# An adaLN block on one core: the order of the projection's passes, planes kept in SBUF, and weight tiles in ten slots

## The chip, the cores and the metric

The kernel runs on one core of a Trainium2 chip. The metric is the device time of one execution in microseconds. A core has five engines that take their instructions in order and meet by semaphores: TensorE (PE, with its weight loads PEld), VectorE (DVE), ScalarE (ACT), GpSimd (POOL) and SyncE (SP), which issues nearly all transfers (DMA) here. SBUF is the on-chip memory, PSUM the accumulator that TensorE writes.

## The reference, cut to what matters

```python
mod = (silu(c) @ w_mod).reshape(1, 6, 1, -1)          # sa, ca, ga, sb, cb, gb
h = layernorm(x) * (1 + ca) + sa
q = (h @ wq) -> 32 heads of 128;  k, v = last 512 keys of 16 cached heads, each for 2 query heads
o = softmax(q k^T / sqrt(128)) v
x = x + ga * (o @ wo)                                  # wo: 4096 x 576
h = layernorm(x) * (1 + cb) + sb
x = x + gb * ((sigmoid(h @ w_gate) * (h @ w_up)) @ w_down)   # 576 -> 4608 -> 576
```

x is 2048 rows of 576, in float32. Every matrix product is made of three products of rounded halves (hi·lo + lo·hi + hi·hi).

## The kernel before

The 2048 rows are four blocks of 512 rows (`xs[0]` to `xs[3]`, four tiles of 128 rows each). Blocks 0 and 1 are pair 0, blocks 2 and 3 pair 1.

**Attention.** 128 block-heads (a block of rows and a head) of four steps each: N = 512 steps, and the table `seq` sets their order; the second half of them, from step n1 = 256 on, treats blocks 2 and 3. A step n makes scores (`st`), their maximum (`neg`), the exponential (`pp`, with its sum), the transposed probabilities split into halves (`ptt`), a quarter of the next q projection (`qp`) and a quarter of the product with v (`ot`). After a block-head's fourth step 1/sum (`rs`) is written to `rscr` in DRAM and read back, spread over all partitions, as `rb` (`put_rs`, `get_rs`); `ov` is `ot` times `rb`, and `put_o` stores it in `oscr`. Work to be done at a given step is entered with `at_n` (ahead of the step's own work) or `at_late` (behind it).

**Beside attention.** The norm of blocks 2 and 3 (`norm_block`, lines from `n1` on: statistics, then a chain of twelve small operations for 1/sqrt, `ln_rsqrt`, then `ln_apply` with GpSimd multiplying by `scale` and adding `shift`). Four modulation rows (`mod_fetch`, `mod_sum`, `mod_make2`). And background jobs, which use the four blocks' rooms in SBUF to combine and split the weights and store them in DRAM: `wsc` and `dsc` for the MLP, `wosc` for the projection.

**Projection.** o @ wo for a pair is computed by a seven-product scheme of Strassen's kind over 2 x 2 halves. A visit takes 8 heads (q, 0 to 3), a pair and a tile t: four sums of o's planes on GpSimd (`v_sum`), seven splits (`v_split`: `vh`, ScalarE and VectorE), and seven stages of 12 matmuls, each closed by one VectorE addition to x (`x<-a,x`, `x<-b,x`, `x<-c,x`; the letter is the PSUM bank). There are 32 visits; q is the outer loop, then the pair, then t. A set of 8 heads has seven weight tiles of 1.18 MB, in eleven slots (`WSLOT`, b0 to b4 and c0 to c5); four sets, 28 loads. `beside(v, s)` says what is issued beside stage s of visit v, its loads included.

**Last visits and MLP.** Pair 0 is complete after visit 28 of 32, counted from 1. In the last four visits its second norm is made (two chains of 13 for blocks 0 and 1, `early_norm`, `early_scale`, `early_sums`), its seven sums (planes B11 to T4) are written to `scr[0]` and read again as `ts` or into xs, and transposed and split (`load_combo`) into `hc`. The MLP then runs u = 0 to 71 (pair 0: 36, pair 1: 36) with seven products of 7 matmuls (`product`; `sr` is the raw weight, `sw` the split one) and the down products (`down`, with `sd`).

**What sets the order.** `pin` and `keep_order` hold an instruction in the order in which it is written on its engine; the rest is placed by a scheduler that knows the dependences. All instructions are issued through the wrapper `Ordered`, so the profile puts them all on line 36, and they are told apart by the names of their tiles.

Of the kernel before, what the change touches and what calls it, by code (L numbers as in the profile page):

```python
# [9 lines left out]
F32 = mybir.dt.float32  # L10
# [34 lines left out]
def adaln_block_kernel(ctx: ExitStack, tc: tile.TileContext, x, k_cache, v_cache, wq, wo, w_gate, w_up, w_down,  # L45
# [85 lines left out]
    ones = wp.tile([P, P], F32, name="ones")  # L131
# [4 lines left out]
    def mod_rows(tag, pool):  # L136
        return pool.tile([P, D], F32, tag=tag, name=tag)

    def mod_load(m):
# [6 lines left out]
        t = wp.tile([TAIL, D], F32, tag="h", name="wmt", bufs=4)  # L146
# [3 lines left out]
    def mod_sum(loaded):  # L150
        ws, t = loaded
        for j in range(2):
            parts = [ws[j][:, k, :] for k in range(NC)] + [t[:, j * D2 : (j + 1) * D2]]
            for k, w in enumerate(parts):
                keep_order(nc.scalar.activation(w, w, AF.Copy, scale=cexp[: w.shape[0], k : k + 1]))
            for w in parts[1:]:
                kk = w.shape[0]
                nc.gpsimd.tensor_add(parts[0][:kk], parts[0][:kk], w)
# [17 lines left out]
    def ln_stats(b, t, hold=False):  # L176
        if t == 0:
            LN[b] = [const.tile([P, TPB, 2], F32, tag="mv", name="mv", bufs=2),
                     const.tile([P, TPB], F32, tag="ln_y", name="ln_y", bufs=2)]
# [8 lines left out]
    def ln_rsqrt(b, part=None, hold=False):  # L188
        mv, y = LN[b][:2]
        if not part:  # L190
            v = const.tile([P, TPB], F32, tag="ln_v", name="ln_v", bufs=2)
            a = const.tile([P, TPB], F32, tag="ln_a", name="ln_a", bufs=2)
            LN[b] += [v, a]
            i = nc.vector.tensor_scalar(v, mv[:, :, 1], EPS, None, op0=OP.add)
            if hold:
                pin(i)
            yi, vi = y.bitcast(I32), v.bitcast(I32)
            nc.vector.tensor_scalar(yi, vi, 1, None, op0=OP.logical_shift_right)
            nc.vector.tensor_scalar(yi, yi, -1.0, float(0x5F3759DF), op0=OP.mult, op1=OP.add)
        v, a = LN[b][2:]  # L200
        for _ in range(3 if part is None else 1):
            nc.vector.tensor_mul(a, y, y)
            nc.vector.scalar_tensor_tensor(a, a, -0.5, v, op0=OP.mult, op1=OP.mult)
            nc.vector.scalar_tensor_tensor(y, a, 1.5, y, op0=OP.add, op1=OP.mult)
# [110 lines left out]
    def ln_ready(b, part=None):  # L315
        ln_rsqrt(b, part)
        if part not in (None, 2):
            return
# [1088 lines left out]
```

## Time and profile before

| | us |
|---|---|
| three runs | 3102.99, 3108.08, 3110.74 (median 3108.08) |
| profiled execution | 3107.64 |
| its span | 3105.9 |
| TensorE busy | 3028.0 (97%) |
| VectorE busy | 2184.5 (70%) |
| ScalarE, GpSimd busy | 1680.7 and 1682.8 (54% each) |
| mean granted TensorE clock | 0.991 |

Attention lasts until about 1444 us, the projection until about 1835 us, the MLP until the end. The granted clock is the share of its full clock that TensorE was given in a stretch. A line of waits names the engine and what it was about to write, then the engine and tile it waited for. In a timeline a row is a start, a length, the engine, the line, the operation, its output and inputs with their shapes, and in brackets the idle time before it and what ended it.

### The profile page before, as it was taken

The page shows a single profiled execution, that of the slowest core. Times are in us where ns is not written, and L with a number is a line of the kernel's source. Part 1 is how long each engine was busy: PE and PEld are TensorE (multiplying, and loading weights), DVE is VectorE, ACT ScalarE, POOL GpSimd, SP SyncE. Part 2 cuts the span into 40 slices and gives each one's busy share as a digit, 9 for nine tenths or more (in the row PEclk, how much of TensorE's full clock was granted, in tenths as well). Part 3 has the DMA queues.
Part 4 walks back from the last instruction along what each step waited for, and adds up shares of the span by engine and source line. Part 5 has one row for each costly group of instructions (what it writes and reads, how often), then busy time and mean ns, then how long its engine had stood idle before and what let it go on. Part 6 is the DMA issues. An engine that isn't in the chain of part 4 may idle for free.

```text
span 3105.9 us, 49158 instructions
## 1 busy us (share of the span) xinstructions
PE 3028.0 (97%) x16635; PEld 2602.8 (84%) x16635; DVE 2184.5 (70%) x3866; ACT 1680.7 (54%) x3356; POOL 1682.8 (54%) x1556
## 2 busy tenths in 40 slices
PE   8999999989999999998999989999999999999998
PEld 6878788867888888887999977888888888888887
DVE  6666666687666666665888977666666776666668
ACT  5666667746667666654343444444454544444543
POOL 2344458744577763112555546666666575655654
PEclk9999999999999999999999999999999999999999
DMA  3677777667677777547545565545545565455453
GB/s 114 186 193 201 203 228 253 227 193 186 198 257 241 249 242 182 145 122 230 186 159 185 175 207 177 167 137 167 180 135 151 163 187 144 138 150 144 139 157 103
DMA packets 471406, 559.27 MB, mean 180 GB/s; under 512 B 51569, under 2 KB 425073, under 8 KB 465649
## 3 DMA queue, kind: packets, MB, share of 16 engines
q1 hardware_dynamic: 470544, 556.11, 60.3%
q8 instruction: 132, 2.16, 0.3%
q14 instruction: 122, 0.99, 0.1%
q10 hardware_dynamic: 608, 0.00, 0.0%
HBM read 384.44 MB, written 171.54 MB: 179 GB/s over the span
## 4 chain that ended last, share of the span: by engine, by line
PE 86%; DVE 5%; DMA 3%; POOL 2%; issue 1%; ACT 1%; SPq 1%; ACTq 0%; DVEq 0%; POOLq 0%
PE a L36 19%; PE st L36 17%; PE qp L36 12%; PE w L36 12%; PE ot L36 10%; PE c L36 10%; PE b L36 5%; DVE x L36 1%; SPq L36 1%; POOL x L36 1%; POOL hl L36 1%; DMA sr<-wsc 1%; DMA raw<-in_A_wq_dram 0%; POOL vs L36 0%; DVE vh L36 0%
## 5 line engine op out<-in xcount | busy, mean ns | idle before, releaser
L36 DVE TENSOR_TENSOR x<-w,x 128x288 f32<-128x288 f32 x980 | 436.4, 453 | 295.6 <-PE w L36 291.8
L36 PE MATMUL a<-hc,sw 128*128 128x512 f32 x2016 | 584.9, 394 | 12.9 <-POOL sw L36 6.5
L36 PEld LDWEIGHTS w<-sd,hl 128*128 128x128 f32 x3036 | 510.7, 188 | 95.4 <-DVE x L36 8.2
L36 PE MATMUL w<-sd,hl 128*128 128x288 f32 x3036 | 563.8, 295 | 6.6 <-DVE x L36 3.7
L36 DVE TENSOR_REDUCE neg<-st 128x1 f32<-128x512 f32 x512 | 352.2, 688 | 283.8 <-PE st L36 283.2
L36 ACT ACTIVATE ptt<-st 128x512 fp32r<-128x512 f32 x512 | 306.2, 598 | 415.1 <-PE st L36 414.9
L36 PE MATMUL ot<-ptt,vs 128*128 128x512 f32 x1536 | 487.0, 425 | 2.5 <-DVE ptt L36 2.4
L36 PE MATMUL st<-kt,qt 128*128 128x512 f32 x1536 | 444.7, 395 | 2.7 <-ACT pp L36 2.7
L36 PE MATMUL qp<-hTm,wa 128*128 128x512 f32 x1536 | 443.6, 397 | 3.8 <-DVE hTm L36 1.9
L36 DVE TENSOR_TENSOR ptt<-st,ptt 128x512 fp32r<-128x512 f32 x512 | 351.7, 687 | 125.5 <-ACT ptt L36 125.1
L36 ACT ACTIVATE sw<-sr 128x384 fp32r<-128x384 f32 x504 | 261.1, 521 | 264.9 <-issue 88.9
L36 PEld LDWEIGHTS a<-hc,sw 128*128 128x128 f32 x2016 | 355.4, 188 | 54.9 <-POOL sw L36 8.1
L36 ACT ACTIVATE pp<-st,neg 128x512 f32<-128x512 f32 x512 | 350.6, 685 | 45.9 <-DVE neg L36 45.4
L36 POOL TENSOR_TENSOR sw<-sr,sw 128x256 fp32r<-128x256 f32 x252 | 205.3, 816 | 307.0 <-ACT sw L36 212.3
L36 PEld LDWEIGHTS qp<-hTm,wa 128*128 128x128 f32 x1536 | 285.0, 189 | 72.7 <-DVE qt L36 6.9
L36 PEld LDWEIGHTS st<-kt,qt 128*128 128x128 f32 x1536 | 288.3, 189 | 68.1 <-ACT pp L36 4.1
L36 PEld LDWEIGHTS st<-ident,pp 128*128 128x128 f32 x2048 | 254.6, 140 | 85.9 <-issue 11.0
L36 PE MATMUL st<-ident,pp 128*128 128x128 f32 x2048 | 308.5, 273 | 13.8 <-DVE rs L36 10.8
L36 POOL TENSOR_TENSOR x<-x 128x256 f32<-128x256 f32 (+3 forms) x334 | 246.8, 758 | 138.2 <-DMA x<-in_B_w_up_dram 88.3
L36 PE MATMUL c<-hc,sw 128*128 128x512 f32 x1008 | 303.2, 394 | 2.0 <-ACT v L36 2.0
L36 PEld LDWEIGHTS ot<-ptt,vs 128*128 128x128 f32 x1536 | 253.1, 191 | 30.1 <-DVE ptt L36 4.3
L36 POOL TENSOR_TENSOR wa<-raw,wa 128x512 fp32r<-128x512 f32 (+1 forms) x128 | 112.2, 876 | 255.8 <-ACT wa L36 221.9
(173 smaller groups left out, 4750.6 us busy)
## 6 DMA issues: line engine op xcount, KB each, us to landing
sr<-wsc SPq DMA_DIRECT2D x504, 192.0 KB
sd<-dsc SPq DMA_DIRECT2D x249, 288.0 KB
dsc<-x SPq DMA_DIRECT2D x34, 1008.0 KB
rb<-rscr SPq DMA_DIRECT2D x128, 256.0 KB
oscr<-ov SPq DMA_DIRECT2D x64, 512.0 KB
vr<-oscr SPq DMA_DIRECT2D x32, 1024.0 KB
wsc<-x SPq DMA_DIRECT2D x36, 896.0 KB
wosc<-x SPq DMA_DIRECT2D x32, 1008.0 KB
```

The source lines that it names most:

```text
L36: i = got(*args, **kw)
```

## The change

1. **Passes.** `PASSES` names (q, pair): (0,0), (0,1), (1,1), (1,0), (2,0), (3,0), (3,1), (2,1). Pair 0 is complete after 24 visits (`DONE0`; visits are counted from 0 from here on). Set 2 is loaded twice: five sets (`WQ`), 35 loads. Pair 0's norm follows in visits 21 to 30: one chain of 13 operations for both blocks (`ln_some`, two per stage), then ten stages for each tile. From visit 25 on two of the four plane sums of a visit are VectorE's.
2. **Planes.** T1, T2 and T4 go to six `ts` tiles, the other four planes lie in xs. `scr[0]` is gone, and with it its stores and loads. The first two combinations are made in visits 30 and 31, and the first eight `sr` loads and four splits stand there.
3. **Ten slots.** Weight tiles live in a0, a1 (a0 is the four `h` rows, a1 the rows `scale`, `shift`, `gate1`, `gate`, all 576 wide), b0 to b2, c0, c1, d0 to d2. A tile is `[P, 4, 2, D2]`, and `wosc` is stored in that order by set and product, so a load reads 9216 contiguous bytes a partition and a store writes pieces of 1152 bytes (8064 before). Set 0's first two tiles are loaded at steps N − 34 and N − 32, three more at N − 6 to N − 4, the last two behind attention. At a set's end four of the next set's seven tiles are loaded as its stages free them, three two visits earlier. The down weights `sd` use seven of the eight rows later.
4. **Last two block-heads.** 1/sum is spread by TensorE: `ident` times `rs` on VectorE (four 128x128), four matmuls with `ones`, one copy on ScalarE. The last `put_o` is issued by ScalarE.
5. **Norm of blocks 2 and 3.** Statistics and loads some steps earlier, the twelve chain operations one per step. The last loads of x come 18 or more steps earlier.
6. **Modulation sums** one row chunk per step instead of all in one.

The diff, cut to its core:

```diff
-    def mod_sum(loaded):
+    def mod_sum(loaded, k):
...
+    def ln_some(b, both, lo, hi, hold=False):
+        for op in ln_chain(b, both)[lo:hi]:
+            i = op()
             if hold:
                 pin(i)
...
-            at_late(n - 1, put_rs, b)
-            at_late(n + 1, get_rs, b)
+            if b < NBLK - 2:
+                at_late(n - 1, put_rs, b)
+                at_late(n + 1, get_rs, b)
+            else:
+                spread_rs(b)
+                at_late(n - 1, spread_mm, b)
...
+    def spread_rs(b):
+        DG[b] = at.tile([P, TPB, P], F32, tag="qt", name="dg", bufs=2)
+        for i in range(TPB):
+            nc.vector.tensor_scalar(DG[b][:, i], ident, RS[b][:, i : i + 1], None, op0=OP.mult)
+
+    def spread_mm(b):
+        p = ps_qp()
+        for i in range(TPB):
+            nc.tensor.matmul(p[:, i * P : (i + 1) * P], ones, DG[b][:, i], start=True, stop=True)
+        RB[b] = at.tile([P, BLK], F32, tag="rb", name="rb", bufs=2)
+        keep_order(nc.scalar.activation(RB[b], p, AF.Copy))
...
-        at_n(N // 2 - 38 + b, load_x, b)
+        at_n(N // 2 - 43 + b, load_x, b)
     for b in range(NB):
-        at_n(N - 30 + 5 * b, load_x, b)
+        at_n(N - 48 + 4 * b, load_x, b)
...
-        at_n(n_stats + TPB, ln_rsqrt, b)
+        for k in range(12):
+            at_n(n_stats + TPB + k, ln_some, b, False, k, k + 1)
...
-    norm_block(2, n1 - 28, n1 - 20, n1 - 14, 2, scale, shift, nc.gpsimd, nc.gpsimd)
-    norm_block(3, n1 - 24, n1 - 8, n1 - 6, 2, scale, shift, nc.gpsimd, nc.gpsimd)
+    norm_block(2, n1 - 35, n1 - 19, n1 - 14, 2, scale, shift, nc.gpsimd, nc.gpsimd)
+    norm_block(3, n1 - 26, n1 - 9, n1 - 6, 2, scale, shift, nc.gpsimd, nc.gpsimd)
...
-    wosc = [dram.tile([P, 2, 4, 7, D2], F32, tag=f"wosc{q}", name=f"wosc{q}") for q in range(H // 8)]
+    wosc = [dram.tile([7, P, 4, 2, D2], F32, tag=f"wosc{q}", name=f"wosc{q}") for q in range(H // 8)]
...
+    PASSES = (0, 0), (0, 1), (1, 1), (1, 0), (2, 0), (3, 0), (3, 1), (2, 1)
+    WQ = 0, 1, 2, 3, 2
+    WOF = 0, 0, 1, 1, 2, 3, 3, 4
...
+    WSLOT = (("a0", "a1", "b0", "b1", "b2", "d0", "d1"), ("d2", "c0", "c1", "a0", "a1", "b0", "b1"),
+             ("b2", "d0", "d1", "d2", "c0", "c1", "a0"), ("a1", "b0", "b1", "b2", "d0", "d1", "d2"),
+             ("c0", "c1", "a0", "a1", "b0", "b1", "b2"))
...
+        eng = nc.vector if v > DONE0 and k % 2 else nc.gpsimd
...
+        if k in (0, 5):
+            v_load(k // 5)
+        if k in (1, 2, 3):
+            w_load(0, k + 1)
+        if 2 <= k < 6:
+            v_sum(0, k - 2)
+        if k in (6, 7, 8):
+            v_split(0, k - 6)
+
+    for s in range(2):
+        at_n(N - 34 + 2 * s, w_load, 0, s)
...
+        k = WOF[v // TPB]
+        if k + 1 < len(WQ):
+            if v == LAST[k] and s < 4:
+                w_load(k + 1, s + 3)
+            elif v == LAST[k] - 2 and s in (1, 3, 5):
+                w_load(k + 1, s // 2)
+        if DONE0 - 4 < v <= DONE0 and s in (0, 2):
+            ln_stats(s // 2, v - DONE0 + 3)
+            park_x(s // 2, v - DONE0 + 3)
+        if v < DONE0:
             return
-        k = 7 * (v - first - 4) + s
...
+        k = 7 * (v - DONE0) + s
+        if 3 <= k < 10:
+            ln_some(0, True, 2 * (k - 3), 2 * (k - 2), True)
+        for t in range(TPB):
+            at = k - 10 - 10 * t
             if at == 0:
                 early_norm(t)
...
+            if at in (1, 3):
+                early_scale(t, at // 2)
+            if 4 <= at < 8:
+                early_sum(t, at - 4)
...
+        if k in (36, 39, 42, 45):
+            split_w()
+            load_w(True)
+        if k in (47, 51):
+            early_stage((k - 47) // 4)
+            load_combo(0, (k - 47) // 4, True)
```

How the order moves, at three places. VectorE near the norm of block 3 in mid-attention, before: the end of the chain (`ln_a`, `ln_y`), which stands in one piece, and the step's work behind it.

```order
L36 SCALAR_TENSOR_TENSOR ln_y<-ln_a,ln_y 128x4
L36 TENSOR_TENSOR ln_a<-ln_y 128x4
L36 SCALAR_TENSOR_TENSOR ln_a<-ln_a,ln_v 128x4
L36 SCALAR_TENSOR_TENSOR ln_y<-ln_a,ln_y 128x4
L36 TENSOR_TENSOR ov<-ot,rb 128x4x128
L36 TENSOR_TENSOR ptt<-st,ptt 128x4x128
L36 RECIPROCAL rs<-sum 128x4
L36 TENSOR_TENSOR ptt<-st,ptt 128x4x128
```

The same engine after the change, between two `ptt`:

```order
L36 TENSOR_SCALAR h<-x_103,mv,ln_y 128x576
L36 TENSOR_REDUCE neg<-st 128x1
L36 SCALAR_TENSOR_TENSOR ln_y<-ln_a,ln_y 128x4
L36 TENSOR_TENSOR ov<-ot,rb 128x4x128
L36 TENSOR_TENSOR ln_a<-ln_y 128x4
L36 TENSOR_SCALAR h<-x_103,mv,ln_y 128x576
L36 SCALAR_TENSOR_TENSOR ln_a<-ln_a,ln_v 128x4
L36 SCALAR_TENSOR_TENSOR ln_y<-ln_a,ln_y 128x4
L36 TENSOR_TENSOR ln_a<-ln_y 128x4
L36 SCALAR_TENSOR_TENSOR ln_a<-ln_a,ln_v 128x4
L36 SCALAR_TENSOR_TENSOR ln_y<-ln_a,ln_y 128x4
L36 TENSOR_REDUCE neg<-st 128x1
```

The chain is cut up by `neg`, `ov` and the `h` that GpSimd multiplies next, and five of its operations still stand together.

SyncE at the end of attention, before (`wb`, `wc` are weight tiles, `vr` the planes of o for a visit):

```order
L36 DMA wb_15318<-wosc_354 128x8x288
L36 DMA rscr_285<-rs 128x4
L36 DMA wb_15353<-wosc_354 128x8x288
L36 DMA rb<-rscr_285 128x512
L36 DMA oscr_3_293<-ov 512x1x256
L36 DMA wb_15380<-wosc_354 128x8x288
L36 DMA wb_15395<-wosc_354 128x8x288
L36 DMA oscr_3_293<-ov 512x1x256
L36 DMA vr<-oscr_0_286 128x2048
L36 DMA wc_15415<-wosc_354 128x8x288
L36 DMA wc_15417<-wosc_354 128x8x288
```

and after:

```order
L36 DMA rb<-rscr_280 128x512
L36 DMA vr<-oscr_0_283 128x2048
L36 DMA wb_15292<-wosc_350 128x2304
L36 DMA wb_15313<-wosc_350 128x2304
L36 DMA wb_15336<-wosc_350 128x2304
L36 DMA vr<-oscr_0_283 128x2048
L36 DMA oscr_3_290<-ov 512x1x256
L36 DMA wd_15437<-wosc_350 128x2304
L36 DMA wd_15439<-wosc_350 128x2304
```

The last two round trips of 1/sum and the last store are gone from this queue, three weight tiles and both `vr` stand ahead of the last store on it, and two tiles (`wd`) behind.

SyncE at the start of the MLP, before:

```order
L36 DMA ts<-scr_294 128x576 x4
L36 DMA scr_294<-x_101 128x288
L36 DMA scr_294<-x_102 128x288 x2
L36 DMA scr_294<-x_101 128x288
L36 DMA sr<-wsc_300 128x384 x4
L36 DMA x_101<-scr_294 128x576 x4
L36 DMA x_102<-scr_294 128x576 x4
L36 DMA ts<-scr_294 128x576 x2
L36 DMA sr<-wsc_300 128x384 x2
L36 DMA sr<-wsc_301 128x384
```

and after, behind the last three weight tiles of the last set:

```order
L36 DMA wb_18985<-wosc_352 128x2304
L36 DMA wb_19005<-wosc_352 128x2304
L36 DMA wb_19026<-wosc_352 128x2304
L36 DMA sr<-wsc_296 128x384 x4
L36 DMA vr<-oscr_2_289 128x2048 x2
L36 DMA sr<-wsc_296 128x384 x2
L36 DMA sr<-wsc_297 128x384
L36 DMA sr<-wsc_296 128x384
```

The stores to and loads from `scr` are gone, and the MLP's weights (`sr`) stand ahead of the last two `vr` instead of behind them.

More of the change, by code (lines that the diff above doesn't have):

```diff
@@ L1031, in load_sd @@
             g, a = sd_uses[i]
-            t = fpool["p"].tile([P, 2, D2], F32R, tag="sd", name="sd", bufs=7)
+            t = flat(const, (["h"] * 4 + ["scale", "shift", "gate1"])[i % 7])
             d = nc.sync.dma_start(f32(t), dsc[g % NG][:, :, a if g == GL else WITH[a]])
@@ L1212, in beside @@
-        if k == 23:
-            for i in range(4):
-                stage_first(i)
-        if k == 26:
-            load_combo(0, 0, True)
+            if at in (1, 3):
+                early_scale(t, at // 2)
+            if 4 <= at < 8:
+                early_sum(t, at - 4)
+        if v == LAST[3] and s == 6:
+            dctx.close()
+            fpool["s"] = ctx.enter_context(tc.tile_pool(name="fs", bufs=1, side="right", reuse_waits="tile"))
+            for _ in range(4):
+                load_w(True)
```

266 lines of the change are left out of this document (119 added, 147 removed).

## The prediction

> **What bounds the kernel now.** I read the page's busy line first, then the windows of 100 us, then the waits of TensorE.
>
> ```profile
> span 3105.9 us, 49158 instructions
> PE 3028.0 (97%) x16635; PEld 2602.8 (84%) x16635; DVE 2184.5 (70%) x3866; ACT 1680.7 (54%) x3356; POOL 1682.8 (54%) x1556
> ```
>
> TensorE is busy for 97% of the span. The change leaves its matmuls as they are (but for eight small ones), so it can win only holes: 3105.9 − 3028.0 = 78 us, and what a lower granted clock costs behind them. The windows (columns: window, length, busy us of PE, PEld, DVE, ACT, POOL, granted clock, DMA share, GB/s) show where they are:
>
> ```profile
> 100.00:200.00 100.00, 97.38 (x500) 79.52 (x498) 65.35 (x104) 65.09 (x147) 43.54 (x56) 1.00 0.74 199
> 600.00:700.00 100.00, 88.25 (x442) 71.77 (x441) 77.80 (x142) 54.53 (x118) 51.88 (x50) 0.95 0.69 198
> 1400.00:1500.00 100.00, 90.39 (x531) 80.36 (x530) 66.04 (x100) 40.63 (x81) 30.47 (x21) 0.93 0.72 234
> 1700.00:1800.00 100.00, 92.22 (x675) 91.24 (x673) 93.69 (x165) 41.33 (x64) 57.28 (x39) 0.98 0.47 163
> 1800.00:1900.00 100.00, 87.78 (x499) 76.88 (x499) 72.16 (x139) 48.02 (x87) 41.97 (x50) 0.95 0.62 201
> ```
>
> Four windows lose 8 to 12 us each: the norm in mid-attention (B), the passage from attention to projection (C), the projection's last visits (D1) and the MLP's start (D2). Elsewhere a window loses 0 to 4. The longest entry of TensorE's waits (us in total, times, longest) is VectorE's, in B:
>
> ```profile
> PE st L36 <- DVE rs L36: 10.8, 2, 9.8
> ```
>
> **B, the norm in mid-attention.** VectorE and GpSimd here:
>
> ```profile
> 663.44 0.16 DVE L36 TENSOR_SCALAR ln_y<-ln_v 128x4 int32<-128x4 int32 x1
> ...
> 676.09 0.56 DVE L36 TENSOR_SCALAR h<-x,mv,ln_y 128x576 f32<-128x576 f32 x1
> ...
> 678.58 1.33 DVE L36 TENSOR_SCALAR ln_y<-ln_v 128x4 int32<-128x4 int32 x1
> ```
> ```profile
> 676.73 3.15 POOL L36 TENSOR_TENSOR h<-h,scale 128x576 f32<-128x576 f32 x2 [4.51 <-DVE h L36]
> 679.85 2.74 POOL L36 TENSOR_TENSOR h<-h,shift 128x576 f32<-128x576 f32 x2
> ```
> ```profile
> 665.00:670.00 5.00, 3.02 (x17) 1.82 (x15) 4.88 (x11) 1.25 (x3) 3.59 (x3) 1.00 1.00 273
> ...
> 675.00:685.00 10.00, 4.17 (x21) 3.10 (x18) 9.68 (x15) 1.74 (x5) 8.19 (x8) 0.90 0.15 44
> 685.00:690.00 5.00, 1.06 (x5) 1.09 (x6) 4.90 (x10) 0.00 (x0) 4.76 (x7) 0.50 0.11 37
> ```
>
> The same 128x4 operation takes 0.16 us alone and 1.33 us while GpSimd multiplies h. Block 3's twelve stand in one row; TensorE idles 1.98 + 5.83 + 3.94 = 11.75 us. The Trainium skill, "SBUF — State Buffer", section "Who interferes with whom", says that VectorE and GpSimd share one port pair, which an instruction locks to its end. The trace agrees (0.16 against 1.33), and by that rule spreading the chain helps only where GpSimd is not at work beside it: the sum would be that of the upper end below.
>
> The change issues the chain one operation per step. But the order of VectorE that results still has ten chain operations (block 2's tail, block 3's head), four h, two neg, one ptt, one qt and one ov between two ptt, and GpSimd's eight h operations belong to just these four h. At most eight chain operations can each meet one of them: 8 × 1.33 + 2 × 0.16 = 11.0; h 4 × 0.56 = 2.2; neg, ptt and qt 4 × 0.69 and ov about 1.1 = 3.9. Sum 17 us.
>
> ```profile
> L36 DVE TENSOR_REDUCE neg<-st 128x1 f32<-128x512 f32 x512 | 352.2, 688 | 283.8 <-PE st L36 283.2
> ```
> ```profile
> 32.60 0.69 DVE L36 TENSOR_REDUCE neg<-st 128x1 f32<-128x512 f32 x1 [1.09 <-PE st L36]
> ...
> 1434.41 1.07 DVE L36 TENSOR_TENSOR ov<-ot,rb 128x512 f32<-128x512 f32 x1
> ...
> 1437.20 0.67 DVE L36 TENSOR_REDUCE neg<-st 128x1 f32<-128x512 f32 x1
> ```
>
> One neg is one step: 512 of them from 32.6 to 1437.2 us make 2.75 us a step. The 17 us serve two steps, and one step of slack lies in the buffers: stall 17 − 8.25 = 8.8 us. None stretched: 7.7 us of work, no stall. I take the upper end, since the order puts them side by side: **gain 3** (11.75 − 8.8), bounds −1 (block 2's tail stretched before it as well) and +12.
>
> **C, attention to projection.** The chain of waits, then the windows:
>
> ```profile
> 1439.18 4.81 DMA rscr<-rs
> ...
> 1444.06 4.35 DMA rb<-rscr
> ...
> 1450.99 10.03 DMA vr<-oscr
> ```
> ```profile
> 1430.00:1440.00 10.00, 9.09 (x52) 7.18 (x51) 9.54 (x16) 7.32 (x19) 5.48 (x4) 1.00 0.66 194
> 1440.00:1450.00 10.00, 6.79 (x40) 5.57 (x38) 3.49 (x6) 1.71 (x3) 0.00 (x0) 1.00 1.01 303
> 1450.00:1470.00 20.00, 14.51 (x63) 12.88 (x64) 7.03 (x13) 3.04 (x5) 5.38 (x4) 0.66 1.06 383
> ...
> 1475.00:1775.00 300.00, 300.00 (x2252) 300.00 (x2251) 261.83 (x401) 118.90 (x188) 166.61 (x107) 1.00 0.54 182
> ```
>
> In the steady projection a matmul takes 300/2252 = 0.133 us, a visit (84) 11.2 us. The 63 matmuls of 1450–1470 are worth 8.4 us, so 11.6 are lost there; with 0.9 and 3.2 ahead, 15.7. The last head's 1/sum goes out and back (9.3 us with its issue), `ov` waits for it, and behind `ov` on VectorE stand the first x and vh of the projection. SP's queue is held by the same trip, so weights and the second vr come late, all at once.
>
> The change fetches two of seven weight tiles some 90 us earlier, in eight pieces, where the DMA has room:
>
> ```profile
> 1300.00:1400.00 100.00, 100.00 (x515) 82.24 (x514) 68.52 (x107) 60.19 (x133) 11.58 (x13) 1.00 0.42 112
> ```
>
> Their rows (h, scale, shift, the gates) were last read by the background jobs and by the norm of mid-attention, so SP, behind which the next heads' rscr and rb stand, should not be held. The change also replaces the round trip of the last two block-heads by four 128x128 products on VectorE (each between the 0.16 and the 0.56 above, say 0.35), four matmuls and one copy on ScalarE:
>
> ```profile
> L36 PE MATMUL st<-ident,pp 128*128 128x128 f32 x2048 | 308.5, 273 | 13.8 <-DVE rs L36 10.8
> L36 ACT ACTIVATE ptt<-st 128x512 fp32r<-128x512 f32 x512 | 306.2, 598 | 415.1 <-PE st L36 414.9
> ```
>
> 1.4 + 0.6 + 0.6 = 2.6 us instead of 9.3, or up to 1.33 × 4 + 1.2 = 6.5 if GpSimd's sums of the first planes meet the products. What remains: two tiles (d0, d1) can only be fetched when attention's pools close. At 383 GB/s a tile of 1.18 MB takes 3.1 us; behind the last `oscr` store d1 lands some 10 to 13 us after the first stage and is due after 9.6: 3 us late. With 2 for the spread and 2 for the clock, 7 stay. **Gain 8.5**, bounds 4 and 13.
>
> **D1, the last visits.**
>
> ```profile
> 1775.00:1835.00 60.00, 47.84 (x326) 46.09 (x324) 51.25 (x92) 22.86 (x35) 29.95 (x27) 0.94 0.46 150
> ```
> ```profile
> 1789.63 3.45 DVE L36 TENSOR_TENSOR x<-x,scale 128x576 f32<-128x576 f32 x2
> ...
> 1801.54 0.74 DVE L36 TENSOR_TENSOR x<-x,scale 128x576 f32<-128x576 f32 x1
> ...
> 1806.69 0.46 DVE L36 TENSOR_TENSOR x<-x 128x288 f32<-128x288 f32 x1 [1.43 <-POOL x L36]
> ```
> ```profile
> L36 DVE TENSOR_TENSOR vh<-vr,vh 128x512 fp32r<-128x512 f32 x108 | 109.2, 1011 | 6.3 <-ACT vh L36 4.8
> ```
>
> 326 matmuls are worth 43.4 us: 16.6 lost. VectorE is busy without a gap while the norm of pair 0 is pressed into four visits. Its steady load is 261.8 us over 2252/84 = 26.8 visits, 9.8 of 11.2 us. The change has eight visits for this work: one chain of 13 operations in place of two (2 per stage in visits 24 and 25), then one tile in 10 stages. Per tile VectorE gets one scale (0.74) and four sums (0.46), 2.6 us in 1.43 visits: 1.8 a visit. It also takes two of four plane sums from GpSimd (about 0.67 each, as a vh alone): 1.3. On the other side vh's mean 1.01 contains contention: 7 × (1.0 − 0.67) = 2.3 us a visit, of which half should go with GpSimd's two sums. 9.8 + 1.8 + 1.3 − 1.2 = 11.7 against 11.2: VectorE is just over, half a us for each of six visits, and about 2 in visit 24 with the chain. Residue 5, bounds 1 and 12; **gain 11.5**, bounds 5 and 16. What is late next is the x add on which stage 2's bank waits: TensorE has one stage, 1.6 us, of slack against it.
>
> **D2, the MLP's start.**
>
> ```profile
> 1835.00:1877.00 42.00, 34.23 (x175) 27.68 (x174) 26.47 (x49) 24.49 (x46) 12.25 (x20) 0.93 0.67 223
> ```
> ```profile
> 1867.08 0.53 SPq L36 DMA_DIRECT2D sd<-dsc  x1
> 1867.71 2.69 SPq L36 DMA_DIRECT2D sr<-wsc  x3
> ```
> ```profile
> PE c L36 <- ACT v L36: 2.0, 1, 2.0
> PE a L36 <- ACT sw L36: 1.5, 1, 1.5
> ```
>
> Idle 7.8, clock 0.07 × 42 = 2.9: 10.7. Before, SP stores and reloads the planes, then waits for a down weight's slot until 1867 with four MLP weights behind it. After, planes stay, eight weights come and four are split in the visits, two combinations of seven are made there, and the slot's wait stands later. Five combinations with their ScalarE and VectorE copies stay in u = 0, and so does part of those waits. **Gain 7.5**, bounds 3 and 11.
>
> **The rest.** Spread modulation sums: 100–200 lost 2.6 us, gain 1.5 (0 to 3). Pair switch with six ts tiles: 0 (−3 to +2). `wosc` stores in pieces of 1152 bytes where 8064 lay in one: 0, beside a DMA that is 0.7 busy in attention (a loss of up to 4 if that cover goes). The seven extra weight tiles are 8.3 MB, on a DMA that is 0.54 busy (1475–1775): 0, but see rival 1. Each of these loads waits on SP for a stage of the visit before, and behind it stands a vr that is due two visits later.
>
> Sum: 3 + 8.5 + 11.5 + 7.5 + 1.5 = 32. The profiled execution took 3107.6 (span 3105.9 and 1.7 around it), 0.5 under the median of the runs: **3075.6, say 3075 us**.
>
> **Rivals.** (1) Late weights, ending slower. At each of four set changes four tiles are fetched only as the last visit frees them, with a vr ahead: 4.72 + 1.05 = 5.77 MB, from 1.6 us into that visit to stage 6 of the next, 19.2 us. That needs 300 GB/s. At the steady 182 GB/s it takes 31.7: 12.5 late, four times 50, result 3125. For it: before, no set was fetched so late. Against: the same queue moved 383 GB/s in 1450–1470, in smaller pieces. (2) VectorE stays the bound in the last eight visits: D1's gain falls away, 3087. For it the sum of 11.7 against 11.2, against it the halved contention. (3) All holes close, B's too: 3075.6 − 8.8 (B) − 7 (C) − 4 (most of D1's rest) = 3056. For it, that the chain was spread; against, VectorE's order. (4) The change does not do what it says in mid-attention: that is already in B.
>
> **How the numbers follow.** My forecast 0.74, (1) 0.06, (2) 0.12, (3) 0.08. Squares of the half-ranges (6, 5, 5, 4, 3) make ±11 around it; with rivals 2 and 3 the range is 3054 to 3097. Against 0.3% (9 us, what a measurement of this kernel can tell from no change), the bound of faster is 3099: the forecast nearly always, rivals 2 and 3 all but always: 0.90. Same 0.05 (forecast at its worst, rival 1 in part), slower 0.05.
>
> **What would show it.** B: neg and ptt without a gap of TensorE near 680 would refute the 8.8; 128x4 operations of 1.3 us confirm it. C: no `rb<-rscr` on the last chain, first visit in under 19 us, waits on wd. D1: VectorE over 95% from the 25th visit on, PE at 0.133 us a matmul but for some 5 us. D2: no ts or x loads, waits on ACT alone. Rival 1 would show as PE waiting for wa or wb every four to eight visits. The prediction is wrong if less than 10 us of the sum comes.

## The result, and the profile after

The changed kernel takes 3082.56 us (median; runs 3081.02, 3083.32, 3081.80 and 3084.14), the kernel before 3109.35 beside it. The ratio is 0.9918, its 95% interval 0.9901 to 0.9935: 25 us faster by the ratio, 27 by the two medians, where 33 had been forecast (3075, range 3054 to 3097). Variants ran on several chips, each beside the kernel before, so they are compared by these ratios; in one run below (all plane sums on VectorE and the norm on GpSimd) the profile fell into an execution in which TensorE was granted a clock of only 0.85 throughout, and no stage of it is read.

The page after, busy line and span:

```profile
span 3079.0 us, 49150 instructions
PE 3022.5 (98%) x16651; PEld 2600.9 (84%) x16651; DVE 2190.9 (71%) x3872; ACT 1680.2 (55%) x3358; POOL 1641.9 (53%) x1534
```

The windows of 100 us that answer to those shown of before (columns: window, length, busy us of PE, PEld, DVE, ACT, POOL, granted clock, DMA share, GB/s):

```profile
100.00:200.00 100.00, 99.51 (x510) 81.49 (x509) 66.72 (x105) 65.85 (x149) 43.42 (x57) 1.00 0.71 191
600.00:700.00 100.00, 92.42 (x459) 75.05 (x458) 76.58 (x146) 53.79 (x120) 38.44 (x42) 0.97 0.66 181
1400.00:1500.00 100.00, 94.90 (x618) 86.96 (x617) 77.80 (x119) 42.62 (x82) 36.65 (x26) 0.98 0.47 167
1700.00:1800.00 100.00, 89.38 (x643) 85.79 (x642) 91.77 (x164) 41.25 (x66) 35.59 (x27) 1.00 0.49 180
1800.00:1900.00 100.00, 97.65 (x563) 85.82 (x562) 78.53 (x158) 55.47 (x103) 51.78 (x57) 1.00 0.51 162
```

Three of the holes are smaller. The one of the last visits is not: 10.6 us are lost between 1700 and 1800. TensorE's longest waits now:

```profile
PE st L36 <- DVE rs L36: 6.4, 1, 6.4
PE c L36 <- DVE x L36: 6.3, 5, 1.9
PE a L36 <- POOL sw L36: 5.2, 3, 1.7
```

A window of fixed time shows other work in the two kernels. So I measured between events that both have: the start of the k-th `neg` (one per step), of TensorE's first matmul of the projection, of `x<-b,x` (one per visit, numbered from 0; it closes the sixth of a visit's seven stages and is called the visit's end below) and of the sigmoid `g<-g` (two per u), all from the timelines. The rows for the last visits, before and after, as an example:

```profile
1725.91 0.46 DVE L36 TENSOR_TENSOR x<-b,x 128x288 f32<-128x288 f32 x1 [0.24 <-PE b L36]
```
```profile
1708.69 0.46 DVE L36 TENSOR_TENSOR x<-b,x 128x288 f32<-128x288 f32 x1
...
1815.55 0.46 DVE L36 TENSOR_TENSOR x<-b,x 128x288 f32<-128x288 f32 x1 [1.13 <-PE b L36]
```

| stretch | before, us | after, us | gain | forecast |
|---|---|---|---|---|
| start to 201st step (the modulation sums in it) | 587.0 | 580.7 | 6.3 | 1.5 |
| 201st to 256th step (B) | 166.1 | 162.7 | 3.4 | 3 |
| 256th to 506th step | 670.7 | 670.9 | −0.2 | 0 |
| 506th step to projection's first matmul (C) | 20.3 | 28.1 | −7.8 | 8.5 with the next |
| first matmul to the first visit's `x<-b,x` (C) | 24.3 | 10.0 | 14.3 | |
| visit 0 to visit 23 | 257.5 | 256.3 | 1.2 | 0 |
| visit 23 to visit 31 (D1) | 106.8 | 106.9 | −0.1 | 11.5 |
| visit 31 to the 13th sigmoid (D2) | 124.6 | 108.5 | 16.1 | 7.5 |
| 13th to 133rd sigmoid | 1029.2 | 1034.0 | −4.8 | 0 |
| 133rd sigmoid to the end of the span | 119.4 | 120.9 | −1.5 | 0 |

They add up to 26.9 us, the difference of the spans. Two combinations of 12 small matmuls, 1.2 us each, moved from the stretch of D2 into that of D1: 2.5 us of D2's gain and of D1's loss are theirs. The start of the first step alone lies between 30.7 and 34.5 us in the profiles of all variants, so the 1.7 us that it gives to the first row are chance; between the first and the 201st `neg` 554.4 became 549.9 here and 550.1 to 552.7 in the other variants whose stages are read, which carry the same edits.

### The profile page after: what moved, and what is told of

Read it like the earlier page. It is cut to its first block, busy times and chain, and to the rows that moved or that the text cites. A ratio compares the mean times of both kernels' runs of the same rounds, so it can differ in the third digit from the quotient of the medians.

```text
span 3079.0 us, 49150 instructions
## 1 busy us (share of the span) xinstructions
PE 3022.5 (98%) x16651; PEld 2600.9 (84%) x16651; DVE 2190.9 (71%) x3872; ACT 1680.2 (55%) x3358; POOL 1641.9 (53%) x1534
## 4 chain that ended last, share of the span: by engine, by line
PE 87%; DVE 5%; POOL 3%; issue 2%; ACT 1%; DMA 1%; SPq 0%; POOLq 0%; ACTq 0%; DVEq 0%
PE a L36 19%; PE st L36 17%; PE qp L36 13%; PE w L36 12%; PE ot L36 11%; PE c L36 10%; PE b L36 5%; DVE x L36 1%; POOL x L36 1%; DVE vh L36 1%; POOL hl L36 0%; PE wo L36 0%; POOL vs L36 0%; DVE neg L36 0%; ACT pp L36 0%
## 5 line engine op out<-in xcount | busy, mean ns | idle before, releaser
L36 POOL TENSOR_TENSOR sw<-sr,sw 128x256 fp32r<-128x256 f32 x252 | 195.0, 775 | 325.1 <-ACT sw L36 228.9
L36 PEld LDWEIGHTS w<-wh,hl 128*128 128x128 f32 x1776 | 299.3, 189 | 54.8 <-DVE x L36 6.0
L36 PE MATMUL w<-wh,hl 128*128 128x288 f32 x1776 | 332.9, 298 | 3.4 <-DVE x L36 3.3
L36 POOL TENSOR_TENSOR hl<-vs,hl 128x512 fp32r<-128x512 f32 x139 | 186.7, 1343 | 98.9 <-ACT hl L36 98.9
```

What stands on the lines that cost most here:

```text
L36: i = got(*args, **kw)
```

## The experiments

All are variants of the changed kernel with its whole computation. Each is given with its time, the ratio to the kernel before beside it, and the stretch in question.

**Who makes the plane sums.** The first run gave them back to GpSimd.

```diff
-        eng = nc.vector if v > DONE0 and k % 2 else nc.gpsimd
+        eng = nc.gpsimd
```

> The changed kernel, but all four plane sums of a visit are GpSimd's again, to the end. In the changed kernel the visits 28 to 30, in which hardly any work of the norm is left, take 12.5 to 13.0 us instead of 11.2, and VectorE waits 0.8 to 1.1 us a visit for GpSimd's first sum. My theory (the two engines hand the sums to and fro, so that VectorE's queue waits and x's addition comes late): visits 28 to 30 go back to 11.2 to 11.5 us; visits 23 to 27 lose 8 to 12 us as before, since contention takes the place of the waits; in all 4 to 6 us faster than the changed kernel, about 3077. Rival (VectorE has simply too much to do from visit 24 on, and the two sums are a part of it): the visits 24 to 27 gain most, 28 to 30 little since there the norm's work is gone; in all 3 to 5 us. Second rival (the sums' place is of no matter, the early weights of the MLP on the DMA queue hold the planes up): within 1 us of the changed kernel, visits 28 to 30 stay at 12.5 or more.

3083.15 us, ratio 0.9932 (0.9917 to 0.9946). Visit 23 to 31 took 105.2 us; visits 28 to 30 took 10.9 to 11.1 each, as my theory had it, but the three before them, 25 to 27, took 16.1, 17.5 and 13.7 in place of 15.2, 15.3 and 12.6. So the handing to and fro is real: in the changed kernel VectorE's queue stood still for GpSimd's sum, and a split that followed was blocked by the next one. VectorE's and TensorE's timelines of the changed kernel show it in a visit with hardly any work of the norm:

```profile
1779.29 0.69 DVE L36 TENSOR_TENSOR vr<-vr 128x512 f32<-128x512 f32 x1 [1.09 <-POOL vt L36]
...
1780.87 1.69 DVE L36 TENSOR_TENSOR vh<-vt,vh 128x512 fp32r<-128x512 f32 x1
```
```profile
1784.21 0.64 PE L36 MATMUL c<-wscale,vh 128*128 128x288 f32 x3 [1.28 <-DVE x L36]
```

But what is won there is lost again where the norm's work stands: the total went nowhere.

The second run gave all of them to VectorE and the norm's scales and sums to GpSimd.

```diff
-        eng = nc.vector if v > DONE0 and k % 2 else nc.gpsimd
+        eng = nc.vector if v > DONE0 else nc.gpsimd
...
-        (nc.vector if b else nc.gpsimd).tensor_mul(h, h, rows2["scale"])
+        nc.gpsimd.tensor_mul(h, h, rows2["scale"])
...
-            nc.vector.tensor_sub(t1, b0, a0)
+            nc.gpsimd.tensor_sub(t1, b0, a0)
```

> The changed kernel, but after pair 0 is complete all four plane sums are VectorE's, and the norm's scales and sums (8 operations per two tiles moved) are GpSimd's. VectorE gets two more operations of 0.68 us a visit, and GpSimd is out of the visits' chain. My theory (handing to and fro): visits 28 to 30 take 11.2 to 11.5 us though VectorE has more to do than in the changed kernel; visits 24 to 27 are 1 to 2 us slower than 11.2 each because the norm's work on GpSimd blocks VectorE's two-input operations; in all 5 to 9 us faster than the changed kernel, about 3075. Rival (too much work on VectorE): visits 28 to 30 are no faster than 12.5 to 13.0, in all the same or 1 to 4 us slower than the changed kernel.

3080.35 us, ratio 0.9918 (0.9902 to 0.9935): the same as the changed kernel, as the rival had it, where I had said 5 to 9 us less. The time alone does not tell which visits made it so; the last run asks again with one edit less.

**The end of attention.**

```diff
-            nc.vector.tensor_scalar(DG[b][:, i], ident, RS[b][:, i : i + 1], None, op0=OP.mult)
+            keep_order(nc.scalar.activation(DG[b][:, i], ident, AF.Copy, scale=RS[b][:, i : i + 1]))
...
-                at_late(n - 1, spread_mm, b)
+                at_late(n, spread_mm, b)
```

> The changed kernel, but the products of ident and 1/sum for the last two block-heads are ScalarE's, and the matmuls and the copy that spread them are issued one step later, so that the last ptt stands ahead of the copy on ScalarE. Between the 506th step and the projection's first matmul the changed kernel needs 28.1 us, the kernel before 20.3. My theory (the eight products are stretched to 0.7 to 0.8 us by GpSimd's plane sums, and the copy, which waits for them, holds the last ptt on ScalarE): 4 to 6 us of these 7.8 come back, the projection's first visit stays without a stall, the clock behind it at full speed; about 3077. Rival (the loss lies in TensorE's extra matmuls and in the clock, whoever makes the products): within 1.5 us of the changed kernel.

3077.80 us, ratio 0.9913 (0.9898 to 0.9928). From the 506th step to the first matmul 21.7 us instead of 28.1, and 9.8 from there to the first visit's end. My theory stands, with 6.4 us at the place. The total shows less, and the ratios cannot tell the two kernels apart: stretches of this profile that the edit does not touch are 1 to 2 us longer (the start, the 201st to 256th step, visits 23 to 31). The changed kernel's ScalarE and TensorE show the knot:

```profile
1436.40 0.60 ACT L36 ACTIVATE rb<-qp 128x512 f32<-128x512 f32 x1 [3.98 <-PE qp L36]
1436.90 0.59 ACT L36 ACTIVATE ptt<-st 128x512 fp32r<-128x512 f32 x1
```
```profile
1435.43 0.94 PE L36 MATMUL qp<-dg,ones 128*128 128x128 f32 x6 [0.73 <-DVE dg L36]
1438.27 4.37 PE L36 MATMUL ot<-ptt,vs 128*128 128x512 f32 x12 [1.90 <-DVE ptt L36]
```

The last `ptt` stands behind `rb` on ScalarE, `rb` waits for TensorE, and TensorE for VectorE's four products. With the edit the last twelve `ot` follow with a shorter wait, and at full pace:

```profile
1433.69 1.06 ACT L36 ACTIVATE ptt<-st 128x512 fp32r<-128x512 f32 x2
1434.65 0.59 ACT L36 ACTIVATE rb<-qp 128x512 f32<-128x512 f32 x1
```
```profile
1435.65 3.06 PE L36 MATMUL ot<-ptt,vs 128*128 128x512 f32 x12 [1.28 <-DVE ptt L36]
```

**The chain in mid-attention.**

```diff
-            at_n(n_stats + TPB + k, ln_some, b, False, k, k + 1)
+            at_n(n_stats + TPB + k, ln_some, b, False, k, k + 1, True)
```

> The changed kernel, but the twelve operations of each chain in mid-attention are held in the order in which they are written, so that they stand one or two to a step, between neg and ptt, and the scheduler can't bunch them. In the changed kernel TensorE idles 7.6 us between 655 and 670 us, 6.4 of it in one piece. My theory (a bunch of five and more operations, each stretched to 1.2 to 1.4 us by GpSimd's h, keeps ptt waiting): the long wait goes, 1 to 2 us of idle time stay, with the clock 6 to 8 us faster than the changed kernel, about 3075. Rival (GpSimd's lock costs the same wherever the chain stands): the idle time stays above 5 us, in pieces of 1 to 2 us, and the time is within 3 us of the changed kernel.

3081.90 us, ratio 0.9920 (0.9904 to 0.9937). From the 201st to the 256th step 158.9 us instead of 162.7. The piece of 6.4 us is gone and the clock stays at 1.00; of 7.6 us of idle time in this stretch 5.1 remain, 3.0 of them between 700 and 710, where GpSimd's h now lies:

```profile
700.00:705.00 5.00, 2.90 (x12) 1.40 (x11) 4.97 (x9) 3.02 (x7) 5.00 (x7) 1.00 0.00 0
705.00:710.00 5.00, 4.08 (x22) 3.15 (x23) 3.60 (x7) 3.35 (x9) 4.84 (x6) 1.00 0.78 232
```

Of the changed kernel the same place:

```profile
660.00:665.00 5.00, 0.00 (x0) 0.00 (x0) 4.86 (x6) 0.00 (x0) 4.84 (x5) 0.98 0.86 228
665.00:670.00 5.00, 3.79 (x11) 3.23 (x12) 3.01 (x6) 2.15 (x6) 3.20 (x5) 0.50 0.37 64
```

So the outcome lies between the two theories. The bunch was worth 3.8 us at the place, half of what I said and too little for the total to show; idle time stays above 5 us, in pieces, and the total within 3 us, as the rival had it.

**The norm in order, plane sums on GpSimd.**

```diff
-        (nc.vector if b else nc.gpsimd).tensor_mul(h, h, rows2["scale"])
+        pin((nc.vector if b else nc.gpsimd).tensor_mul(h, h, rows2["scale"]))
...
-            nc.vector.tensor_sub(t1, b0, a0)
+            pin(nc.vector.tensor_sub(t1, b0, a0))
...
-        eng = nc.vector if v > DONE0 and k % 2 else nc.gpsimd
+        eng = nc.gpsimd
```

> The changed kernel, but the norm, scales and sums of pair 0 in the last eight visits are held in the order in which they are written, so that they spread over the visits 25 to 30 as the code says, where the scheduler had drawn them into visits 24 to 27; and all plane sums are GpSimd's, as in the run with that alone. From visit 23 to 31 the kernel before and the changed one both need 106.8 us, the run with the plane sums on GpSimd 105.3, of which 13.8 us too many in visits 23 to 27 and none in 28 to 30; eight steady visits and two combinations would be 91.6. My theory (two causes: handing to and fro, and the drawing together): 95 to 98 us from visit 23 to 31, no visit over 12.5, about 8 us faster than the changed kernel. Rival (VectorE's load is too high wherever the work stands): 103 to 107 us, the loss only spread evenly over the visits 24 to 30.

3083.32 us, ratio 0.9927 (0.9910 to 0.9943). Visit 23 to 31: 108.4 us; the visits from 25 to 30 took 14.9, 13.0, 12.8, 13.3, 13.8 and 15.7 (the last has one of the combinations in it). The theory of two causes fell, and the rival came, a little above its range: the loss is only spread. What VectorE pays is in the groups of its splits: 0.67 to 0.69 us alone, about 1 us beside GpSimd's sums. In this run, in visits 23 to 31:

```profile
L36 DVE TENSOR_TENSOR vh<-vr,vh 128x512 fp32r<-128x512 f32 x31 | 30.5, 983 | 1.9 <-ACT vh L36 1.9
L36 DVE TENSOR_TENSOR vh<-vt,vh 128x512 fp32r<-128x512 f32 x24 | 24.2, 1009 | 3.1 <-ACT vh L36 2.9
```

**The round trip and the early weights.**

```diff
-            if b < NBLK - 2:
+            if b < NBLK:
...
```

> The changed kernel, but the last two block-heads' 1/sum goes through DRAM again as before; the early weights, the last store on ScalarE's queue and all the rest stay. It tells which part made the projection's start 14 us shorter (first matmul to the first visit's end: 24.3 us before, 10.0 in the changed kernel). My theory (the early weights and planes did it; the spread through TensorE cost time where it stands): from the 506th step to the first matmul 20 to 23 us instead of 28.1, from the first matmul to the first visit's end 11 to 15, in all the same as the changed kernel or up to 6 us faster. Rival (the round trip held VectorE and the DMA queue, as the prediction said): the first visit's end falls back by 8 us or more.

3080.85 us, ratio 0.9923 (0.9908 to 0.9938). From the 506th step to the first matmul 20.3 us, from there to the first visit's end 14.9: 35.2 in all, against 38.1 in the changed kernel, 31.4 with the spread on ScalarE and 44.6 before. So the spread through TensorE, as it was built, cost 2.9 us more than the round trip; the other edits of this place (early weights, the order on SyncE's queue, the last store) gave 9.4. The round trip does hold VectorE, 3.4 us of it:

```profile
1443.86 3.25 PE L36 MATMUL a<-wb,vh 128*128 128x288 f32 x12 [3.42 <-DVE x L36]
```

```diff
-    for s in range(2):
-        at_n(N - 34 + 2 * s, w_load, 0, s)
...
-        if k in (1, 2, 3):
-            w_load(0, k + 1)
+        if k in (1, 2, 3, 4, 6):
+            w_load(0, (1, 2, 3, 4, 6).index(k))
```

> The changed kernel, but the first two weight tiles are loaded with the other three in attention's last seven steps, not 30 steps earlier. Spread through TensorE and all the rest stay. My theory (the early weights are what lets the first visit run without a stall): the first visit's end comes 4 to 8 us later, with TensorE waiting on weight tiles. Rival (the order of the DMA queue without the round trip is enough, 383 GB/s being plenty): the first visit takes 10 to 12 us as in the changed kernel, the time is within 1 us of it.

3084.53 us, ratio 0.9933 (0.9918 to 0.9948). From the 506th step to the first visit's end 41.2 us instead of 38.1: 3.1, less than I said, and TensorE waits for splits of the second visit's planes, not for weights. The event overstates the loss: here the scheduler put the first visit's sixth stage, which the event closes, behind the second visit's first one; up to the end of visit 23 it is 295.6 us against 294.4, a loss of 1.2. One of the waits for splits:

```profile
1454.39 0.40 PE L36 MATMUL a<-wh,vh 128*128 128x288 f32 x1 [0.72 <-ACT vh L36]
```

So of the 9.4 us 1 to 3 are the early weights'. The rest was not tried by itself; the earlier planes, the order on SyncE's queue and the last store on ScalarE's are what is left for it.

**Places in SBUF.** From u to u the steady MLP has the same matmuls in the same order and no wait on TensorE in the kernel before and the changed one (only the down weights lie in other tiles), and yet a u took 16.853 us before and 16.947 after (the mean of 20 u, from the 81st sigmoid to the 121st), and 16.94 to 16.95 in every variant that keeps the changed kernel's places. TensorE is busy without a gap in both, at a granted clock of 1.00, with fewer matmuls in the same time after:

```profile
2600.00:2900.00 300.00, 300.00 (x1622) 262.52 (x1621) 198.74 (x401) 147.51 (x276) 175.27 (x162) 1.00 0.51 144
```
```profile
2600.00:2900.00 300.00, 300.00 (x1613) 262.26 (x1612) 199.05 (x399) 146.80 (x275) 171.87 (x160) 1.00 0.50 143
```

```diff
-    warm = const.tile([P, 1], F32, name="warm")
+    warm = ident[:, :1]
...
+    hp.tile([P, 8], F32, name="pad")
```

> The changed kernel, but a small tile at the start of SBUF shares the place of another, so that everything behind it lies 32 bytes lower, and the rows of the MLP's weights and activations begin at multiples of 64 bytes. In the changed kernel one u of the MLP takes 16.947 us where it took 16.853 before (72 of them: 6.8 us lost), though TensorE waits for nothing and has the same matmuls; a down product whose two operands lie 64 bytes apart (modulo 128) takes 135.9 ns from start to start, one whose operands lie alike 132.5, before 131.6. My theory (TensorE's pace depends on where the operands begin): a u takes 16.85 us or less, the projection's visit changes too, 5 us or more faster. Rival (it is the number of semaphores or the order in which the matmuls stand): 16.94 to 16.95 us a u as in the changed kernel.

3082.59 us, ratio 0.9928 (0.9913 to 0.9942). A u took 16.927 us, 0.02 less, and a visit 11.11, which lies within what the profiles of the changed kernel's layout show (11.06 to 11.15): the pace does depend on places, but multiples of 64 are not what it wants, and the effect was a fifth of what I said.

**Together.** The chain in order, the spread on ScalarE, the norm held in order, and all plane sums on VectorE.

```diff
-        eng = nc.vector if v > DONE0 and k % 2 else nc.gpsimd
+        eng = nc.vector if v > DONE0 else nc.gpsimd
```

> The changed kernel with three edits together: the chain of mid-attention held in its order, the spread of 1/sum on ScalarE and a step later (both as tried alone), and in the last eight visits the norm's operations held in their order while all four plane sums of a visit are VectorE's, with the norm's scales and sums divided as in the changed kernel. The run with the norm held and all plane sums on GpSimd needed 108.4 us from visit 23 to 31, so order alone did not help. My theory now (what VectorE loses is the time in which GpSimd's plane sums block its two-input operations, about 0.33 us of each vh and up to 1.2 us of a single one, more than the 0.68 us that a plane sum costs VectorE itself): VectorE has 7 vh and 7 additions, 6.8 us a visit, four sums 2.7 and the norm's share 1.8, 11.3 us with hardly any blocking; 94 to 99 us from visit 23 to 31 instead of 106.8, and with 6.5 us at attention's end and 3.8 in mid-attention about 18 us faster than the changed kernel, 3062 to 3068. Rival (VectorE's count of operations is what binds, whoever blocks whom): 106 us or more from visit 23 to 31, in all 3071 to 3076.

3062.36 us, ratio 0.9860 (0.9845 to 0.9874). Visit 23 to 31: 95.6 us, 11.2 fewer than the changed kernel; from the 506th step to the first visit's end 31.4 us, 6.7 fewer; from the 201st to the 256th step the 3.8 fewer of the chain alone. The splits between visit 23 and 31 are unblocked, though VectorE makes four sums more a visit than before the change:

```profile
L36 DVE TENSOR_TENSOR vh<-vr,vh 128x512 fp32r<-128x512 f32 x33 | 23.1, 701 | 1.1 <-ACT vh L36 1.1
L36 DVE TENSOR_TENSOR vh<-vt,vh 128x512 fp32r<-128x512 f32 x24 | 16.4, 684 | 0.4 <-ACT vh L36 0.2
```

The rival, that the number of VectorE's operations binds, is out.

```diff
-        pin((nc.vector if b else nc.gpsimd).tensor_mul(h, h, rows2["scale"]))
+        pin(nc.gpsimd.tensor_mul(h, h, rows2["scale"]))
...
-            pin(nc.vector.tensor_sub(t1, b0, a0))
+            pin(nc.gpsimd.tensor_sub(t1, b0, a0))
```

> As the run before, but the scales and sums of the norm in the last visits are GpSimd's (eight operations more per two tiles there), so that VectorE has only its 7 vh, 7 additions and four plane sums, 9.5 us a visit, while GpSimd's large operations stand beside it. My theory (blocking costs VectorE more than the operations would): slower than the run before by 3 to 8 us between visit 23 and 31, 98 to 104 us. Rival (the count of operations binds): faster than the run before there, 92 to 96 us.

3068.01 us, ratio 0.9881 (0.9865 to 0.9898). Visit 23 to 31: 102.4 us. Taking 20 operations of the norm from VectorE, five a tile, made these visits 6.8 us longer. It was busy 94.3 us instead of 92.1, with fewer operations, and stood still for 8.2 instead of 3.5: beside GpSimd's large operations, both its own operations and its waits grow by more than it was spared.

The combined run again, with two small tiles in the places of others, so that the rows begin 32 bytes behind a multiple of 128, as before the change:

```diff
-    warm = const.tile([P, 1], F32, name="warm")
+    warm = ident[:, :1]
...
-    cexp = const.tile([P, NC + 1], F32, name="cexp")
...
+    small = const.tile([P, NC + 10], F32, name="small")
+    cexp = small[:, : NC + 1]
...
-    fcol = const.tile([P, 3, 3], F32, name="fcol")
+    fcol = small[:, NC + 1 :].rearrange("p (a b) -> p a b", a=3)
...
+    hp.tile([P, 16], F32, name="pad")
```

> The combined run with all plane sums on VectorE, and beside it only other places in SBUF: two small tiles share the place of others, so that the rows of the MLP's weights and activations begin 32 bytes behind a multiple of 128 as in the kernel before (96 behind in the changed one, 64 in the run with everything 32 bytes lower). From u to u TensorE's instructions and semaphores are the same in the kernel before and the changed one; a u took 16.853 us before, 16.947 in the changed kernel and in every variant of it, 16.927 with everything 32 bytes lower. My theory (the places set TensorE's pace): 16.85 to 16.87 us a u, the projection's visit goes back from 11.14 towards 11.20, 4 to 6 us faster than the combined run, 3056 to 3060. Rival (something else between the kernels, such as the transfers beside it, sets the pace): 16.92 to 16.95 us a u, the same time as the combined run.

3055.74 us, ratio 0.9840 (0.9825 to 0.9854), the fastest version. A u takes 16.840 us, a hair less than before the change, and the window has its matmuls again:

```profile
2600.00:2900.00 300.00, 300.00 (x1624) 262.47 (x1623) 195.85 (x402) 147.21 (x276) 176.54 (x161) 1.00 0.50 143
```

The visit did not go back towards the 11.20 of before, as I had said; it took 11.11, so nothing shows that places set the pace of the projection. In the MLP they do set TensorE's pace: nothing else differs between this run and the combined one. By what rule, and whether it is the places of TensorE's own operands or of the others', stays open.

The last run: the changed kernel and all plane sums on VectorE, nothing else.

> The changed kernel with one edit: once pair 0 is complete, all four plane sums of a visit are VectorE's, where they were divided between the two engines. The norm's operations stay where the scheduler put them, in visits 24 to 27. It divides the combined run's gain between visits 23 and 31 (106.8 to 95.6 us). My theory (blocking by GpSimd's sums and the waits for them make up nearly all of it, the order little): 96 to 99 us. Rival (the held order is half of it): 100 to 104 us, with the loss in visits 24 to 27.

3073.53 us, ratio 0.9893 (0.9877 to 0.9910), 97.7 us from visit 23 to 31. One line brings 9.1 of the 11.2 us there; the norm's order brings 2.1 when it is held as well.

## Why the prediction was right and wrong

The direction and the places of the holes were right, and the whole came out near the forecast; three terms were wrong. That the whole came so near is in part luck: D1 gave 11.6 us less than its term and the steady MLP and the end lost 6.3 that stood in no term, while D2 gave 8.6 more and the start, chance included, 4.8 more.

**B was right, for its reason.** Forecast 3 us, 3.4 measured. The chain did meet GpSimd's h in the row that the order showed, and the operations are as long as said:

```profile
660.85 1.32 DVE L36 SCALAR_TENSOR_TENSOR ln_y<-ln_a,ln_y 128x4 f32<-128x4 f32 x1
662.20 0.16 DVE L36 TENSOR_TENSOR ln_a<-ln_y 128x4 f32<-128x4 f32 x1
662.40 1.25 DVE L36 SCALAR_TENSOR_TENSOR ln_a<-ln_a,ln_v 128x4 f32<-128x4 f32 x1
```

The stall was forecast as 8.8 us instead of 11.75; it is 6.4 at the place, and 7.6 with two short waits elsewhere in the stretch. The Trainium skill, "SBUF — State Buffer", section "Who interferes with whom", on the port pair that VectorE and GpSimd share, agrees with these rows (0.16 against 1.25 to 1.32 us).

**C came to 6.5 instead of 8.5, and the working was wrong on both sides.** The start of the projection won 14.3 us, more than forecast: d0 and d1 came in time. The end of attention lost 7.8. I had priced the spread at 2.6 us, or 6.5 if GpSimd met the products; it did meet them:

```profile
1421.34 3.22 DVE L36 TENSOR_SCALAR dg<-ident,rs 128x128 f32<-128x128 f32 x4
...
1433.07 2.70 DVE L36 TENSOR_SCALAR dg<-ident,rs 128x128 f32<-128x128 f32 x4
```

But the step that failed is "1.4 + 0.6 + 0.6 = 2.6 us instead of 9.3": it set the new chain against the old one and did not ask what stands behind the copy on ScalarE. That was the last `ptt`, which the round trip had never held. In the run with late weights the last four products met no sum and took 0.86 us in all, and the stretch to the first matmul was still 26.4 us; with the products on ScalarE and the copy behind the last `ptt` it was 21.7. So the copy's place seems to be the larger part, though no run moves it alone.

**D1 failed.** "9.8 + 1.8 + 1.3 − 1.2 = 11.7 against 11.2" gave a gain of 11.5; there was none, or 2.4 us if the two combinations that moved into these visits are left out (rival 2, to which I had given 0.12, forecast just this stretch; its 3087 missed the total since D2 gave more). The load was right: eight visits of 11.7 us and 2 for the chain are 95.6, and VectorE was busy 95.6. The step that failed is the one from the load to the time. It takes VectorE's queue as never standing still ("VectorE is busy without a gap", where the row beside it has 51.25 of 60 us), and the queue stood still for 11.3 of the 106.9 us. The stretch in the changed kernel, and in the one with all plane sums on VectorE and nothing else:

```profile
1708.69:1815.55 106.86, 96.24 (x698) 92.65 (x697) 95.58 (x172) 45.97 (x74) 31.63 (x27) 1.00 0.49 175
```
```profile
1711.01:1808.73 97.72, 94.46 (x698) 93.39 (x697) 93.69 (x185) 45.97 (x74) 12.83 (x13) 0.98 0.53 192
```

With all sums on it VectorE makes 14 sums more, is busy 1.9 us less and stands still 7.3 us less. Alternating one chain of four sums between two engines adds waits that no sum of durations shows: 0.8 to 1.1 us of VectorE's queue in four of the visits, 3.5 us in all. Most of the rest of the 11.3 us are waits for ScalarE and TensorE, whose origin I did not trace. The halved contention ("of which half should go") came in part: the splits' means, 1.01 us (of `vr`) and 0.94 (of `vt`) in the steady projection before, are 0.76 and 0.97 in these visits, 0.76 and 0.78 with all sums on VectorE, 0.70 and 0.68 with the norm held in order as well. The runs weigh the whole: sums undivided on VectorE 97.7 us, divided 106.9, undivided on GpSimd 105.2. That the scheduler draws the norm's work into visits 24 to 27 was in the order and not in my sum; holding it in order gained 2.1 us with the sums on VectorE and lost 3.2 with them on GpSimd.

**D2 was the right mechanism, sized too small.** The term was 10.7 us to be lost in 1835–1877, of which 7.5 to come back; 16.1 came, 2.5 of it the moved combinations. The window was too short: the MLP's first six u, to 1957 us, were still being held in the kernel before (two sigmoids a u; from the first to the 13th 104.1 us became 95.8). And nearly all that was lost came back, not two thirds of it: in the whole stretch TensorE was idle for 10.8 us before and for 2.4 after, and its clock went from 0.97 to 1.00. The stretch before and after:

```profile
1832.69:1957.29 124.60, 113.82 (x594) 95.82 (x593) 87.80 (x188) 65.40 (x123) 69.06 (x73) 0.97 0.60 191
```
```profile
1815.55:1924.07 108.52, 106.17 (x571) 91.30 (x570) 81.01 (x169) 59.56 (x113) 65.31 (x66) 1.00 0.55 175
```

No run takes these edits back, so how the gain divides between the planes kept, the early weights and splits, and the later wait for a down weight's slot is argued from the order and not shown.

**The rest.** The stretch with the modulation sums gave 1.7 to 4.5 us from the first to the 201st step in the profiles of the changed kernel and its variants, where 1.5 was forecast; no run tries these sums alone. The 4.8 us that the steady MLP lost were in no term and in no rival. Rival 1 (late weights) did not happen: visits 0 to 23, with three changes of sets in them, took 11.14 us each, and TensorE's list of waits has no weight tile of the projection.

## What to carry to other kernels

A chain of small steps that passes from one in-order engine to another and back can cost a queue waits that its busy time does not show; where GpSimd's large operations stand beside VectorE's two-input ones, moving work from GpSimd to the busier VectorE can make VectorE's part shorter. When a transfer is replaced by work on engines, look at what stands behind each new instruction on its queue, not only at the length of the new chain. To see what a reordering did, measure between events that both kernels have, stretch by stretch: gains here were up to 16 us and losses up to 8, and cancelled in part within the total.

## What the runs showed of the hardware that I had not expected

TensorE's pace in the MLP changed with the places of the tiles in SBUF, with the same matmuls in the same order, no wait and a granted clock of 1.00: 16.853, 16.947, 16.927 and 16.840 us a u in four layouts (0.6% between the ends). Nine profiles of variants with the changed kernel's layout give 16.94 to 16.95 as the mean, though these differ in other stages. Over 60 u the 0.094 us between the first two make 5.6, enough for the 4.8 us that the stretch from the 13th to the 133rd sigmoid lost; with only the places changed, that stretch went from 1034.5 us in the combined run to 1028.8. That is more than many a hole that was worked on.
